# Cluster attention with a mixer: when a weight's absolute value is issued, and when U's tiles are cleared

## The chip, the cores and the metric

The kernel runs on one core of a Trainium2 chip. The metric is the device time of one execution in microseconds (us), as the median of several runs. Five engines work side by side, each through its own instructions in order: TensorE (PE, its weight loads are PEld), VectorE (DVE), ScalarE (ACT), GpSimd (POOL) and SyncE (SP), which issues every transfer of this kernel. They wait for each other by semaphores.

## What is computed

The reference in short: a clustered attention, a mixing block and a second mixing block with a feed-forward.

```
mask   = argmax(q_n @ c_n) == argmax(k_n @ c_n)           # 16 clusters a head
attn   = softmax(where(mask, q @ k.T / 8, -1e9)) @ v      # 2 x 8 heads, 768 x 64
x      = attn with the heads side by side                 # 2 x 768 x 512
theta  = x @ w_theta
u      = x + w_tok_r @ (x * cos(theta)) + w_tok_i @ (x * sin(theta))
x2     = u + relu(u @ w_ch)
u2     = x2 + (x2.T @ U @ V).T
out    = u2 + relu(u2 @ w_ch1) @ w_ch2
```

All weights come from memory as 64-bit floats and are turned into pairs of 32-bit tiles on the chip, while other work runs.

## The kernel before

**Stages.** A prologue, then attention over eight groups g0 to g7 (two heads of one batch row each), then the mixer: 24 steps that each make one block of theta (`theta`, L476), its cosine and sine, and z (`theta_z`, L496, `theta_lo`, L502), and two steps later the products with w_tok_r and w_tok_i (`ymix`, L518). Then come w_ch, U and V, and the feed-forward.

**A group** has six slots, p0 to p5. In a slot PE forms score tiles `st` for this group (L301), ACT takes their exponentials `p` (L306, four instructions a slot), and PE forms scores `smax` of the next group (L249), whose row maxima `mx` DVE reduces (L253, three a slot). Two products `pv` of exponentials and values (L314) follow, and at p1 and p5 the sums of the exponentials, `l` (L333: at p5 over the tiles of its first three key blocks, at p1 of the next group over the rest). PE works through this in the order written, and that order doesn't change.

**What is fitted in between.** At the end of a slot `fill(1.7)` issues side work until a running account, `owed`, is used up: first the items in `bg` (splitting q and k of a later group into high and low part, L186 on ACT and L191 on POOL; assigning clusters, `sims`, `amax`, `eq`, `weigh`, `least`, `onehot`, `turn`, L122 to L150 on DVE), and then steps of the conversion of a weight, `conv_step`, at a cost of 1 each.

**A weight's conversion** (`Convert`): its load by SP into a staging tile `st` (`load`, L374; two such buffers, so a new load is issued once a weight has gone through `low`); `magnitude` on ACT (absolute value, L382, `cv<-st`); `bits` (L386), `top` (L390) and `low` (L394) on DVE; then, as callbacks that are issued at the end of a slot's scores, `wh` on ACT (L399) and `wl` on POOL (L403). Before the change `magnitude` of the following weight is issued right behind `low` of the one before. During attention (`held[0]`) the order of weights is wth0 to wth2 (theta), then wr0, wi0, wr1, wi1, ... wr5, wi5.

**Buffers.** The tiles `p`, `cv`, `wh`, `wl`, `lt` and many others come from one pool of 59 slots, handed out in the program's order; a tile that takes a slot waits until the last reader of the tile that held it is done. PE's results go to eight banks in a ring, two of them kept by `pv`; a matmul that takes a bank waits for the last reader of what it held. Six banks turn round, and a slot takes three for `st` and three for `smax`, so `l` at the end of a slot takes the bank of that slot's first `st`, and can start once the first exponential of the slot has read it.

**U.** U's conversion ends in five callbacks, one to a `conv_step`: `keep_u0` clears four tiles `ub` on POOL (L560), then `keep_u` four times, each with four small copies on ACT (L567).

Of the kernel before, what the change touches and what calls it, by code (L numbers as in the profile page):

```python
# [10 lines left out]
F32 = mybir.dt.float32  # L11
# [9 lines left out]
B, H, S, D, C = 2, 8, 768, 64, 16  # L21
DM, RANK, DFF = 512, 32, 2048
P = 128
# [17 lines left out]
def tile_cluster_block(ctx: ExitStack, tc: tile.TileContext, qk, v, cent, wth, wr, wi, wch,  # L41
                       u_in, v_in, w1, w2, cst, out):
    nc = tc.nc
# [7 lines left out]
    def slot(name, dt=F32, shape=None):  # L51
        return sp.tile(shape or [P, S], dt, tag="slot", name=name)
# [265 lines left out]
    def pv_out(g):  # L318
        xT[g] = slot(f"xT{g}")
        for hf in range(2):  # L320
            nc.scalar.activation(out=xT[g][:, cols(hf)], in_=pvt[g][hf][:, :HALF], func=AF.Copy)
        give("pv")
# [35 lines left out]
    def norm_x(g):  # L358
        nc.vector.tensor_tensor(xT[g], xT[g], rl.pop(g), op=ALU.mult)


    class Convert:
# [5 lines left out]
            self.c0, self.w = i * S, min(S, n - i * S)  # L368

        def load(self):  # L370
            self.st = stg.tile([P, S, 2], I32, tag="st", name="st")
            for g in range(self.copies):
                r = slice(g * self.rows, (g + 1) * self.rows)
                nc.sync.dma_start(out=self.st[r, :self.w].rearrange("p n t -> p (n t)"),  # L374
                                  in_=self.src[:, self.c0:self.c0 + self.w].bitcast(I32))
            self.part = slice(0, self.copies * self.rows)
            self.hw, self.lw = self.st[self.part, :self.w, 1], self.st[self.part, :self.w, 0]
# [28 lines left out]

    conv_load, conv_in, conv_do, conv_after = deque(), deque(), deque(), deque()
    held = [False]

    def conv_start():  # L410
        while conv_load and len(conv_in) < 2:
            c = conv_load.popleft()
            c.load()
            conv_in.append(c)

    def conv_step(n=1):

        for _ in range(n):
            if conv_after and not held[0]:
                conv_after.popleft()()  # L420
            if not conv_do:
                conv_start()
                if not conv_in:
                    return
                c = conv_in[0]

                def last(c=c):
                    c.low()
                    conv_in.popleft()
                    conv_after.extend([lambda f=f: f(c) for f in c.done])  # L430
                    if conv_in:
                        conv_in[0].magnitude()
                    conv_start()

                conv_do.extend((c.bits, c.top, last))
                if c.t is None:
                    conv_do.appendleft(c.magnitude)
            conv_do.popleft()()

    def conv_until(dst, i):  # L440
        while i not in dst:
            assert conv_do or conv_in or conv_load or conv_after
            conv_step()
# [110 lines left out]
    ub = []  # L554
    vs = []

    def keep_u0(c):
        for i in range(4):
            t = slot(f"ub{i}", F32, [P, 6, P])
            nc.gpsimd.memset(t, 0.0)  # L560
            ub.append(t)

    def keep_u(c, g):
        z = c.t.rearrange("p (k r) -> p k r", r=RANK)
        r = slice(32 * g, 32 * g + 32)
        for i in range(4):
            nc.scalar.activation(out=ub[i][r, :, r], in_=z[r, 6 * i:6 * i + 6], func=AF.Copy)  # L567
        if g == 3:
            uv["u"] = True
# [101 lines left out]
    bg = deque()  # L671

    owed = [0.]

    def fill(t):

        owed[0] += t
        while owed[0] > 0:
            if bg:
                c, f = bg.popleft()  # L680
                f()
                owed[0] -= c
            else:
                conv_step()
                owed[0] -= 1.

    PAUSE = (1, lambda: None)

# [6 lines left out]
    def attention():  # L695


        ORDER = [(0, 0), (0, 2), (0, 4), (1, 0), (1, 2), (1, 4)]
        pvq = deque()
        held[0] = True  # L700

        def next_pv():
            g, kt, hf = pvq.popleft()
            pv(g, kt, hf)
            if kt == NT - 1 and hf:
                pv_out(g)

        for g in range(NG):
            nxt = g + 1 < NG
            if nxt:  # L710
                load_v(g + 1)
            if g + 2 < NG:
                if g > 0:
                    bg.extend(split_items(g + 2, nc.gpsimd))
                bg.extend(assign_items(g + 2))
            if g + 4 < NG:
                for i in range(2):
                    load_raw(g + 4, i)
            if g == 1:
                conv_load.extend(weigh_in(wth, NP * DM, wth_t))  # L720
                conv_start()
            if g == 2:
                tok = [c for p in zip(weigh_in(wr, NT * S, wr_t), weigh_in(wi, NT * S, wi_t)) for c in p]
                conv_load.extend(tok[:6])
                late = tok[6:]
            if g == 6:
                conv_load.extend(late)
                conv_start()
            if g in (6, 7):
                for t in range(2):  # L730
                    bg.append((0, lambda t=2 * g - 12 + t: split_x(0, t, nc.gpsimd)))
            order = [None, (1, 0), None, (1, 2), None, (1, 4)] if g == 0 else ORDER
            for p in range(NT):
                ready = len(pvq)
                if order[p]:
                    h, a = order[p]
                    scores_pair(g, h, a)
                    if h:
                        pvq.extend((g, kt, hf) for kt in (a, a + 1) for hf in range(2))
                if nxt:  # L740
                    max_pair(g + 1, p // 3, 2 * p % 6)
                    if p % 3 == 2:
                        max_join(g + 1, p // 3)

                while conv_after:
                    conv_after.popleft()()
                if p == 3 and g + 2 < NG:
                    mask_rows(g + 2)
                if g > 0 and p == 1:
                    sum_keys(g - 1, 1)  # L750
                if p == 5:
                    sum_keys(g, 0)
                for _ in range(min(ready, 2)):
                    next_pv()
                if g > 0 and p == 1:
                    row_sums(g - 1)
                if g > 0 and p == 5:
                    bg.appendleft((.95, lambda: norm_x(g - 1)))
                    bg.appendleft((.97, lambda: spread(g - 1)))
                fill(1.7 if nxt else 3.4)  # L760
                if g > 0 and p == 0:
                    max_rows(g, 1)
                if nxt and p == 3:
                    max_rows(g + 1, 0)
            while bg:
                fill(.5)
        held[0] = False
        while len(pvq) > 1:
            next_pv()
        nc.scalar.activation(out=warm, in_=warm, func=AF.Sin)  # L770
        next_pv()
        sum_keys(NG - 1, 1)
# [96 lines left out]
    def mixer():  # L869
# [4 lines left out]
        for n in range(len(seq) + LEAD):  # L874
            if n < len(seq):
                theta(*seq[n])
                conv_step()
                theta_z(*seq[n])
            if n >= LEAD:
                ymix(*seq[n - LEAD])  # L880
            if n == 1:
                row_sums(last)
            if n == 2:
                spread(last)
                norm_x(last)
            if n not in range(16, 20):
                conv_step()
            if n < len(seq):
                theta_lo(*seq[n])
            if n not in range(16, 20):  # L890
                conv_step(1)
            if n in (9, 10):
                for t in range(2):
                    split_x(1, 2 * (n - 9) + t)
            if n == 12:
                conv_load.extend(weigh_in(wch, NP * DM, wch_t))
                c1, c2 = weigh_in(w1, NF * DM, w1_t), weigh_in(w2, NF * DM, w2_t)
                conv_load.extend([c1[0], c2[0]])
                conv_load.append(Convert(u_in, S, 0, [keep_u0] + [lambda c, g=g: keep_u(c, g) for g in range(4)], 32, 4))
                conv_load.append(Convert(v_in, S, 0, [keep_v, keep_vl], 32))  # L900
                for p in zip(c1[1:], c2[1:]):
                    conv_load.extend(p)
                conv_start()
            if 20 <= n <= 23:
                split_x(0, n - 20, nc.gpsimd)
            if n in (24, 25):
                split_x(1, n - 24, nc.gpsimd)
# [101 lines left out]
```

## Time and profile before

| | |
|---|---|
| Median of three runs | 729.67 us (727.72 to 731.31) |
| Span of the profiled execution | 725.5 us, 10613 instructions |
| Busy share of the span | PE 96%, PEld 75%, DVE 60%, ACT 41%, POOL 27% |
| Granted clock of TensorE, mean | 0.988 of full speed |

The span runs from the first to the last instruction of the one execution that was profiled. The profile gives no other time of that execution; the median of the runs stands 4.2 us above its span, which holds what lies around it. An engine's share is an average over stages in which different engines wait.

### The profile page before, as it was taken

The numbers are of one execution on the slowest core, as the hardware profiler recorded it, in microseconds if no ns is written. First come the engines' busy times: TensorE is split into PE (matmuls) and PEld (weight loads), VectorE is DVE, ScalarE is ACT, GpSimd is POOL, SyncE is SP. The second block draws the span as 40 slices with busy tenths as digits, with TensorE's granted clock in tenths as the row PEclk, the third lists the DMA queues.
The fourth block names the chain that finished last, engine by engine and source line by source line (L and its number), as shares of the span: only waits on it lengthen the run. The fifth ranks groups of instructions, "written<-read, shape, count | busy, mean of one in ns | idle before, by whom it ended". The sixth has DMA issues, their size and how long they took to land.

```text
span 725.5 us, 10613 instructions
## 1 busy us (share of the span) xinstructions
PE 696.6 (96%) x4109; PEld 546.2 (75%) x4110; DVE 436.5 (60%) x746; ACT 301.0 (41%) x613; POOL 196.7 (27%) x191
## 2 busy tenths in 40 slices
PE   6699989999999899999998899999999999999997
PEld 2455554554555479999998899898888888888986
DVE  7777986878788645447677877644344453332222
ACT  5655644665667644354546712422222222110000
POOL 9602313142244722112346712321221211100000
PEclk9799999999999999999999999999999999999999
DMA  7969666465423400000222211022121221100112
GB/s 210 238 177 262 171 147 186 126 161 151 112 82 127 140 37 1 2 1 30 88 54 89 88 44 44 0 88 74 58 87 51 81 87 30 30 1 0 59 38 79
DMA packets 21506, 64.05 MB, mean 88 GB/s; under 512 B 4272, under 2 KB 6192, under 8 KB 21456
## 3 DMA queue, kind: packets, MB, share of 16 engines
q1 hardware_dynamic: 21456, 63.37, 30.5%
q8 instruction: 32, 0.52, 0.3%
q14 instruction: 18, 0.15, 0.1%
HBM read 40.94 MB, written 3.15 MB: 61 GB/s over the span
## 4 chain that ended last, share of the span: by engine, by line
PE 86%; DVE 7%; ACT 3%; issue 2%; DMA 1%; POOL 0%; SPq 0%; DVEq 0%; ACTq 0%; POOLq 0%
PE g L633 19%; PE acc L653 18%; PE y L518 11%; PE st L301 9%; PE pv L314 8%; PE l L333 5%; PE h L536 5%; PE smax L249 4%; PE th L476 4%; DVE mx L253 2%; PE h L588 1%; DMA st<-in_wr_dram 1%; DVE tht L484 1%; PE sims L119 1%; PE th L480 1%
## 5 line engine op out<-in xcount | busy, mean ns | idle before, releaser
L403 POOL TENSOR_TENSOR wl<-cv,wh 128x768 fp32r<-128x768 f32 (+1 forms) x40 | 79.3, 1982 | 223.7 <-ACT wh L399 195.9
L640 DVE SCALAR_TENSOR_TENSOR gl<-g,gh 128x512 fp32r<-128x512 f32 x48 | 33.2, 692 | 155.7 <-ACT gh L638 155.7
L638 ACT ACTIVATE gh<-g 128x512 fp32r<-128x512 f32 x48 | 28.7, 599 | 202.0 <-PE g L633 202.0
L306 ACT ACTIVATE p<-st 128x512 f32<-128x512 f32 x192 | 78.9, 499 | 65.8 <-PE st L301 59.2
L253 DVE TENSOR_REDUCE mx<-smax 128x1 f32<-128x512 f32 x144 | 90.1, 683 | 20.4 <-PE smax L249 20.4
L518 PE MATMUL y<-wh,z 128*128 128x384 f32 x384 | 89.0, 344 | 4.5 <-ACT z L496 4.5
L633 PE MATMUL g<-uh,wh 128*128 128x512 f32 (+1 forms) x256 | 86.9, 339 | 0.0
L633 PE MATMUL g<-uh,wl 128*128 128x512 f32 (+1 forms) x256 | 86.5, 338 | 0.0
L633 PE MATMUL g<-ul,wh 128*128 128x512 f32 (+1 forms) x256 | 86.1, 337 | 0.0
L301 PE MATMUL st<-qp,kp 128*128 128x256 f32 (+1 forms) x384 | 81.7, 355 | 0.5 <-ACT p L306 0.5
L301 PEld LDWEIGHTS st<-qp,kp 128*128 128x128 f32 x384 | 56.0, 191 | 26.6 <-issue 10.2
L653 PE MATMUL acc<-gh,wh 128*128 128x512 f32 x192 | 75.9, 395 | 0.0
L653 PE MATMUL acc<-gh,wl 128*128 128x512 f32 x192 | 75.6, 394 | 0.0
L653 PE MATMUL acc<-gl,wh 128*128 128x512 f32 x192 | 75.3, 392 | 0.0
L314 PE MATMUL pv<-p,v 128*64 128x384 f32 x384 | 71.6, 498 | 1.4 <-ACT p L306 1.4
L518 PEld LDWEIGHTS y<-wh,z 128*128 128x128 f32 x384 | 67.9, 191 | 5.1 <-ACT z L496 5.1
L633 PEld LDWEIGHTS g<-ul,wh 128*128 128x128 f32 x256 | 48.5, 189 | 6.5 <-POOL ul L616 0.4
L633 PEld LDWEIGHTS g<-uh,wl 128*128 128x128 f32 x256 | 48.4, 189 | 5.8
L633 PEld LDWEIGHTS g<-uh,wh 128*128 128x128 f32 x256 | 48.4, 189 | 5.7
L314 PEld LDWEIGHTS pv<-p,v 128*64 128x64 f32 x384 | 23.6, 136 | 37.6 <-issue 34.4
L518 PE MATMUL y<-wl,z 128*128 128x384 f32 x192 | 49.5, 339 | 0.0
L394 DVE SCALAR_TENSOR_TENSOR cv<-st,cv 128x768 int32<-128x768 int32 (+2 forms) x42 | 45.1, 1075 | 0.9
(129 smaller groups left out, 1177.0 us busy)
## 6 DMA issues: line engine op xcount, KB each, us to landing
st<-in_w_dram SPq DMA_DIRECT2D x20, 768.0 KB, 4.2
raw<-in_qk_dram SPq DMA_DIRECT2D x16, 384.0 KB, 4.7
qp<-hi SPq DMA_DIRECT2D x30, 192.0 KB, 3.0
st<-in_wr_dram SPq DMA_DIRECT2D x6, 768.0 KB, 4.3
st<-in_wi_dram SPq DMA_DIRECT2D x6, 768.0 KB, 4.3
kp<-hi SPq DMA_DIRECT2D x32, 96.0 KB, 3.0
qp<-lo SPq DMA_DIRECT2D x32, 96.0 KB, 2.9
v<-in_v_dram SPq DMA_DIRECT2D x8, 384.0 KB, 3.6
```

Of the source, the lines that this page charges most:

```text
L253: nc.vector.tensor_reduce(mx_t[g, h][:, o:o + n], ps.rearrange("p (n w) -> p n w", n=n), axis=AX.X, op=ALU.max)
L301: nc.tensor.matmul(out=ps[:, c:c + n], lhsT=kp[s, h, w][:, (a + j) * P:(a + j + 1) * P], rhs=qp[s, h, w][:, q0:q0 + n], start=(w == 0), st ...
L306: nc.scalar.activation(out=pt[g, h, a + j][:, q0:q0 + n], in_=ps[:, c:c + n], func=AF.Exp, scale=float(D) ** -0.5)
L314: nc.tensor.matmul(out=pvt[g][hf][64 * h:64 * h + 64, :HALF], lhsT=v_t[g][:, kt, 64 * h:64 * h + 64], rhs=pt[g, h, kt][:, hf * HALF:(hf + ...
L333: nc.tensor.matmul(out=ps[o:o + 32, :HALF], lhsT=ones, rhs=pt[g, h, kt][:, cols(hf)], start=(kt == 3 * a), stop=(kt == 3 * a + 2))
L394: nc.vector.scalar_tensor_tensor(t, self.lw, 29, t, op0=ALU.logical_shift_right, op1=ALU.bitwise_or)
L403: nc.gpsimd.tensor_tensor(t[:, :c.w], c.t, f32(c.hi[:, :c.w]), op=ALU.subtract)
L518: nc.tensor.matmul(out=yps[u, j][hf][:, :HALF], lhsT=lhs, rhs=w[st][e][:, hf * HALF:(hf + 1) * HALF], start=(st == 0 and n == 0), stop=(st ...
L536: nc.tensor.matmul(out=ps[hf][:, :HALF], lhsT=wv[a], rhs=xs[b, t][c][:, hf * HALF:(hf + 1) * HALF], start=(n == 0), stop=(n == 11))
L633: nc.tensor.matmul(out=ps[:, o:o + w], lhsT=wv[a], rhs=us[b, t][e][:, s0:s0 + w], start=(n == 0), stop=(n == 11))
L640: nc.vector.scalar_tensor_tensor(gl, ps, 0.0, f32(gh), op0=ALU.max, op1=ALU.subtract)
L653: nc.tensor.matmul(out=aps[c, e], lhsT=wv[a], rhs=g[x], start=(first and i == 0), stop=(last and i == 2))
```

## The change

Four things are done. `conv_magnitude`, at the head of every attention slot, issues the absolute value of the weight in front, if its load was issued at least two slots before (`RIPE`); behind `low` it is no longer issued while attention runs, and `conv_step` does nothing, and says so, when the front weight has no absolute value yet. `fill` then stops, and carries over at most 1 (`OWED`) of its account. The first load of w_tok, wr0, is issued at the head of g2, beside wth2. And the tiles `ub` are cleared one by one in steps 13 to 16 of the mixer, so U's callbacks are four.

```diff
         def load(self):
+            self.at = tick[0]
...
     held = [False]
+    tick = [0]
+    RIPE = 2
+
+    def conv_magnitude():
+        if conv_in and conv_in[0].t is None and tick[0] - conv_in[0].at >= RIPE:
+            conv_in[0].magnitude()
...
                 conv_start()
-                if not conv_in:
-                    return
+                if not conv_in or held[0] and conv_in[0].t is None:
+                    return False
...
                     conv_after.extend([lambda f=f: f(c) for f in c.done])
-                    if conv_in:
+                    if conv_in and not held[0]:
                         conv_in[0].magnitude()
...
             conv_do.popleft()()
+        return True
...
-    def keep_u0(c):
-        for i in range(4):
-            t = slot(f"ub{i}", F32, [P, 6, P])
-            nc.gpsimd.memset(t, 0.0)
-            ub.append(t)
+    def clear_u(i):
+        t = slot(f"ub{i}", F32, [P, 6, P])
+        nc.gpsimd.memset(t, 0.0)
+        ub.append(t)
...
+    OWED = 1.
     def fill(t):
...
+            elif conv_step():
+                owed[0] -= 1.
             else:
-                conv_step()
-                owed[0] -= 1.
+                owed[0] = min(owed[0], OWED)
+                return
...
                 late = tok[6:]
+                conv_start()
...
                 ready = len(pvq)
+                tick[0] += 1
+                conv_magnitude()
...
-                conv_load.append(Convert(u_in, S, 0, [keep_u0] + [lambda c, g=g: keep_u(c, g) for g in range(4)], 32, 4))
+                conv_load.append(Convert(u_in, S, 0, [lambda c, g=g: keep_u(c, g) for g in range(4)], 32, 4))
...
+            if 13 <= n <= 16:
+                clear_u(n - 13)
```

In the listings below a row is the line of the kernel, the operation, and output and inputs with the number of the tile; lines behind L366 stand one higher after the change (the absolute value is L382 before and L383 after).

ACT in g2, from the mask rows of p4 on, before; `st_1263` is the staging tile of wr0, the first piece of w_tok_r:

```order
L282 ACTIVATE qp001_86<-mrow_1266 2x384 x2
L306 ACTIVATE p1_1275<-st_1277 128x512
L306 ACTIVATE p1_1275<-st_1281 128x256
L306 ACTIVATE p1_1276<-st_1281 128x256
L306 ACTIVATE p1_1276<-st_1288 128x512
L399 ACTIVATE wh_1302<-cv_928 128x768
L382 ACTIVATE cv_1314<-st_1263 128x768
L306 ACTIVATE p1_1318<-st_1320 128x512
L306 ACTIVATE p1_1318<-st_1324 128x256
```

ACT at the same place after the change; wr0's staging tile is `st_1047` there, loaded at the head of the group:

```order
L282 ACTIVATE qp001_86<-mrow_1274 2x384 x2
L383 ACTIVATE cv_1283<-st_1047 128x768
L306 ACTIVATE p1_1285<-st_1287 128x512
L306 ACTIVATE p1_1285<-st_1291 128x256
L306 ACTIVATE p1_1286<-st_1291 128x256
L306 ACTIVATE p1_1286<-st_1298 128x512
L400 ACTIVATE wh_1312<-cv_981 128x512
L306 ACTIVATE p1_1324<-st_1326 128x512
```

The absolute value stood behind p4's exponentials and `wh`, ahead of p5's exponentials; it stands now at the head of p4, and the `wh` of a weight of theta between the two groups of exponentials.

DVE in g1, from the join of the maxima in p2 to the maxima of p4, before; `cv_885` is wth0, the first piece of theta's weight:

```order
L269 TENSOR_TENSOR m2_882<-mx_880,m2_882 128x6
L386 TENSOR_SCALAR cv_885<-cv_885 128x768
L253 TENSOR_REDUCE mx12_905<-smax_906 128x1
L253 TENSOR_REDUCE mx12_905<-smax_909 128x2
L253 TENSOR_REDUCE mx12_905<-smax_913 128x1
L390 SCALAR_TENSOR_TENSOR cv_885<-st_707,cv_885 128x768
L394 SCALAR_TENSOR_TENSOR cv_885<-st_707,cv_885 128x768
L253 TENSOR_REDUCE mx12_905<-smax_958 128x1
L253 TENSOR_REDUCE mx12_905<-smax_961 128x2
```

And after the change, with `cv_791` for wth0 and `cv_892` for wth1:

```order
L269 TENSOR_TENSOR m2_885<-mx_883,m2_885 128x6
L391 SCALAR_TENSOR_TENSOR cv_791<-st_707,cv_791 128x768
L395 SCALAR_TENSOR_TENSOR cv_791<-st_707,cv_791 128x768
L253 TENSOR_REDUCE mx12_911<-smax_912 128x1
L253 TENSOR_REDUCE mx12_911<-smax_915 128x2
L253 TENSOR_REDUCE mx12_911<-smax_919 128x1
L387 TENSOR_SCALAR cv_892<-cv_892 128x768
L391 SCALAR_TENSOR_TENSOR cv_892<-st_709,cv_892 128x768
L253 TENSOR_REDUCE mx12_911<-smax_964 128x1
```

One conversion step stood ahead of p3's maxima (`smax_906` to `smax_913`) and two behind them; now two stand ahead (`smax_912` to `smax_919`) and two behind.

ACT in g4, p4 and the beginning of p5, before; `cv_1987` and `cv_1889` are wi1 and wr1, `p1_1991` the first exponentials of p5:

```order
L306 ACTIVATE p1_1954<-st_1959 128x256
L306 ACTIVATE p1_1954<-st_1966 128x512
L382 ACTIVATE cv_1987<-st_1891 128x768
L306 ACTIVATE p1_1991<-st_1993 128x512
L306 ACTIVATE p1_1991<-st_1997 128x256
L306 ACTIVATE p1_1992<-st_1997 128x256
L306 ACTIVATE p1_1992<-st_2004 128x512
L399 ACTIVATE wh_2023<-cv_1889 128x768
```

And after the change; `cv_1956` is wi1, `cv_1660` wr1, and `p1_1997` the first exponentials of p5, whose slot is the one that `cv_1660` held:

```order
L383 ACTIVATE cv_1956<-st_1658 128x768
L306 ACTIVATE p1_1958<-st_1960 128x512
L306 ACTIVATE p1_1958<-st_1964 128x256
L306 ACTIVATE p1_1959<-st_1964 128x256
L306 ACTIVATE p1_1959<-st_1971 128x512
L400 ACTIVATE wh_1985<-cv_1660 128x768
L306 ACTIVATE p1_1997<-st_1999 128x512
L306 ACTIVATE p1_1997<-st_2003 128x256
```

wi1's absolute value moved ahead of p4's exponentials, and wr1's `wh` from behind p5's exponentials to ahead of them; POOL's `wl` of wr1 reads `cv_1660` behind that `wh`.

## Rows read from the trace of the kernel before

**Rows 1.** the page: span, and shares of the chain that ended last

```profile
span 725.5 us, 10613 instructions
...
PE 86%; DVE 7%; ACT 3%; issue 2%; DMA 1%; POOL 0%; SPq 0%; DVEq 0%; ACTq 0%; POOLq 0%
```

**Rows 2.** timeline, all engines, 108 to 112 us: start, length, instruction [idle before <-releaser]

```profile
109.04 0.89 ACT L382 ACTIVATE cv<-st 128x768 f32<-128x768 f32 x1 [4.14 <-DMA st<-in_wr_dram]
...
110.46 3.84 PE L333 MATMUL l<-p,ones 128*32 128x384 f32 x24 [3.74 <-ACT p L306]
```

**Rows 3.** windows: stretch, busy (x) PE PEld DVE ACT POOL, PEclk, DMA, GB/s

```profile
110.40:114.30 3.90, 3.84 (x26) 1.08 (x28) 0.00 (x0) 1.56 (x5) 1.26 (x1) 0.56 0.96 387
```

**Rows 4.** chain in order of time, g0: start, length, engine, line

```profile
45.43 1.81 DVE mx L253 x3
```

**Rows 5.** timeline of DVE in g0

```profile
47.76 0.57 DVE L150 STREAM_TRANSPOSE eqw<-eqw 128x384 bf16<-128x384 bf16 x1
```

**Rows 6.** timeline of g1, 70 to 82 us

```profile
72.84 1.88 DVE L253 TENSOR_REDUCE mx<-smax 128x1 f32<-128x512 f32 x3
...
74.64 0.95 DVE L390 SCALAR_TENSOR_TENSOR cv<-st,cv 128x768 int32<-128x768 int32 x1
...
75.06 1.51 PE L314 MATMUL pv<-p,v 128*64 128x384 f32 x8
...
78.30 1.57 DVE L386 TENSOR_SCALAR cv<-cv 128x768 int32<-128x768 int32 x1
```

**Rows 7.** timeline of g4, 144 to 172 us

```profile
146.64 3.63 POOL L191 TENSOR_TENSOR lo<-raw,hi 128x768 fp32r<-128x768 f32 x2 [5.78 <-ACT hi L186]
...
150.38 2.14 PE L333 MATMUL l<-p,ones 128*32 128x384 f32 x24
...
163.97 1.64 ACT L306 ACTIVATE p<-st 128x512 f32<-128x512 f32 x4
...
167.69 2.14 PE L333 MATMUL l<-p,ones 128*32 128x384 f32 x24
...
168.73 1.81 POOL L403 TENSOR_TENSOR wl<-cv,wh 128x768 fp32r<-128x768 f32 x1 [5.63 <-ACT wh L399]
```

**Rows 8.** timeline of g5, 165 to 190 us

```profile
178.77 0.56 DVE L130 TENSOR_TENSOR eqw<-s_t,mxc 128x384 bf16<-128x384 f32 x1 [0.62 <-POOL lo L191]
...
180.07 2.14 PE L333 MATMUL l<-p,ones 128*32 128x384 f32 x24 [1.72 <-ACT p L306]
```

**Rows 9.** timeline of g6, 214 to 228 us

```profile
216.90 1.88 DVE L253 TENSOR_REDUCE mx<-smax 128x1 f32<-128x512 f32 x3
...
218.21 1.83 POOL L403 TENSOR_TENSOR wl<-cv,wh 128x768 fp32r<-128x768 f32 x1 [3.85 <-issue]
...
218.69 2.17 DVE L390 SCALAR_TENSOR_TENSOR cv<-st,cv 128x768 int32<-128x768 int32 x1
...
224.97 2.14 PE L333 MATMUL l<-p,ones 128*32 128x384 f32 x24
```

**Rows 10.** chain in order of time, g7

```profile
238.34 0.23 DVE rl L343
...
240.44 4.12 DMA st<-in_wr_dram
```

**Rows 11.** timeline of g7

```profile
240.29 0.55 DVE L386 TENSOR_SCALAR cv<-cv 128x768 int32<-128x768 int32 x1
...
246.02 1.51 PE L314 MATMUL pv<-p,v 128*64 128x384 f32 x8 [1.36 <-ACT p L306]
```

**Rows 12.** timeline of the mixer's steps 21 to 23

```profile
388.49 3.35 POOL L560 MEMSET ub<- 128x768 f32 x4
...
391.07 0.73 ACT L496 ACTIVATE z<-tht 128x256 fp32r<-128x256 f32 x2 [0.75 <-DVE tht L493]
...
391.71 2.24 ACT L567 ACTIVATE ub<-cv 32x192 f32<-32x192 f32 x8
...
400.90 1.01 PE L518 MATMUL y<-wh,z 128*128 128x384 f32 x2 [4.21 <-ACT z L496]
```

## The prediction

> **What bounds the kernel now.** I read the page first. The chain of work that ended last is 86% PE [rows 1]: over most of the 725.5 us PE is never short of work, and nothing done beside it counts. So the change is worth what it does to the few places where PE waits, and I went through attention group by group with the timeline to find these, then through the chain of waits to see what ended each. The largest by far is in g2 at p5. ACT's absolute value of wr0 stood idle for 4.14 us for its load, and p5's exponentials stand behind it on ACT. PE's `l` needs the bank that the first of them frees, so it waited 3.74 us [rows 2]. Behind that wait the granted clock of the stretch was 0.56, near the lower level of 1.2 GHz [rows 3], and this `l` took 3.84 us where the one of g4 takes 2.14 [rows 2, 7]. Smaller ones: 1.72 in g5 [rows 8], 1.36 in g7 [rows 11], and 4.21 in the mixer's step 23 [rows 12]. In g0 the chain goes through DVE's maxima [rows 4].
>
> I then put the rows of the change's order against these times: which instruction stands ahead of which, what held the slot or the bank that an instruction takes, and when that came free.
>
> **The change part by part.** Nothing is computed more or less, except that the four clears are on other steps. Everything is a question of who stands in front of whom.
>
> A, g2 p5. wr0 is now loaded at the head of g2 and its absolute value issued at p4's head, four slots behind. The wait goes, and the slow `l` with it: 3.74 + (3.84 - 2.14) = **-5.4**. If a wait of the size of those in g5 or g7 comes in its place, -3.7; nothing suggests more than -5.4.
>
> B, g0. The account starts one higher, so the item `turn` (0.57, [rows 5]) moves ahead of the maxima of p2, which are on the chain there [rows 4]: **+0.5**, from 0 to 0.6.
>
> C, g1. The assignment's items stand in p0 now but for one, and wth0's conversion begins a slot earlier. So `top` and `low` of wth0, 0.95 each [rows 6], stand ahead of p3's maxima where `bits` (0.55, [rows 11]) stood: 1.35 more. DVE also reaches this place some 0.3 later, since the items drawn forward push its work for `l` and p2's maxima back (an estimate: they are a little over 1 us, and most of it is idle time of DVE there). Before, those of p3 ended at 72.84 + 1.88 = 74.72, and p4's `pv`, which takes the bank of the third of them, started at 75.06 [rows 6]. The maxima would end at 74.72 + 1.65 = 76.4 and `pv` start then: +1.3. Behind it `bits` and `top` of wth1 stand ahead of p4's maxima, the first stretched to 1.57 beside POOL's `wl` as it was at 78.30 [rows 6], which puts p5's `smax` back by another 0.7 (1.57 + 0.95 ahead of maxima that stood free, less what `st` of p5 and PE's own delay cover, some 1.8). Together **+2.0**. The low end is 0.2, if the banks have more slack than this counting gives; the high end 2.6.
>
> D, g4 p1. The first exponential now takes a slot that POOL's second `lo` reads last, until 146.64 + 3.63 = 150.27. With the 0.5 that the first exponential of a group of four needs (estimate from 1.64 for four) `l` could start at 150.8 and started at 150.38 [rows 7]: **+0.4**, from 0 to 0.6.
>
> E, g4 p5. The first exponential takes the slot of wr1's `cv`, whose `wh` now stands right ahead of it and whose `wl` is POOL's. p4's exponentials end at 163.97 + 1.64 = 165.6, `wh` takes 0.9 like the absolute value of [rows 2], `wl` 1.81, the exponential 0.5: 168.8, against `l` at 167.69 [rows 7]. **+1.2** with the hand-over between engines, from 0 (PE itself late by then) to 1.6.
>
> F, g5 p1. The first exponential waited for the slot that DVE's `eq` read; `eq` had itself waited for POOL's `lo` and took 0.56 from 178.77 [rows 8]. After the change that slot waits for `lo` alone: **-0.6**. At best the whole wait of 1.72 goes, at worst nothing.
>
> G, g6 p5. wr4's load is issued behind `low` of wr3, which now stands behind p3's maxima. These end at 216.90 + 1.88 = 218.8 [rows 9], I take 219.0; `low` is done at 220.0. The load lands 4.12 later, like the one of [rows 10], at 224.1; 0.9 of absolute value at p5's head and 0.5 of exponential make 225.5, against `l` at 224.97 [rows 9]: **+0.6**, from 0 to 1.6. Here the rule "two slots old" does not help: p3 to p5 is two slots, and they last less than load and conversion.
>
> H, g7. The chain before runs from DVE's sums over wr/wi conversions into the load of the last weight, 4.12 [rows 10], and PE's `pv` waits 1.36 [rows 11]. After the change wi4's three steps begin when the sums are through, at 238.6 [rows 10], and take 0.55 + 0.95 + 0.95: the load leaves at 241.1 instead of 240.44 and lands at 245.2. The absolute value stands at p3's head and blocks ACT as before, so the wait becomes about 2.0. Some of the 0.6 comes back, since no further absolute value stands ahead of p4's exponentials: **+0.3**, from -1.8 (no wait at all) to +0.9.
>
> I, the mixer. Clearing cost POOL 3.35 for four [rows 12], and PE did not wait for it. In steps 13 to 16 the clears lie in POOL's idle time, one a step, 0.8 each. But U's callbacks come one `conv_step` sooner: half of the eight copies of 2.24 us, 1.1, now stand on ACT ahead of step 22's z, where ACT was idle for only 0.75 [rows 12]. The rest, 0.4, is passed on to step 23, whose wait of 4.21 becomes 4.6: **+0.4**, from -0.3 to +0.8. That wait itself is not touched.
>
> Sum: -5.4 + 0.5 + 2.0 + 0.4 + 1.2 - 0.6 + 0.6 + 0.3 + 0.4 = **-0.6**. The span of 725.5 becomes 724.9. The median of the runs stands 4.2 above the span of the profiled execution, so about **729.1**: the one big wait goes, and small ones take its place. With all terms at their low ends the sum is -8.9, at their high ends +5.0.
>
> **The rule that speaks against it.** At 218.69 DVE's `top` took 2.17, where the same instruction takes 0.95 elsewhere [rows 6, 9]; POOL's `wl` of 1.83, begun at 218.21, ran beside it [rows 9]. The Trainium skill says ("SBUF — State Buffer", section "SBUF: two separate sides") that DVE and GpSimd share one pair of ports as an exclusive lock, so the one that starts second stands for the other's whole instruction; the 2.17 agrees with that. In G, plain durations give +0.6; a step blocked as at 218.69 would issue the load up to 1.2 later, about half of it in time in which DVE would wait anyway (an estimate), so +1.2, and the sum would be 0.0 instead of -0.6.
>
> **The rivals.**
>
> 1. *The new waits don't bite.* Slots and banks have more slack than the counting gives, DVE makes up in its idle time, and only A and F remain: -6.0, **723.7**. For it: each of B to E is 2 us or less, and each is counted from the ends of single instructions. Against it: g0 and g1 have DVE on the chain already [rows 4], and D and E follow from one buffer's last reader.
>
> 2. *Slower: POOL's `wl` becomes the last reader in front of the exponentials.* Place: g4 p5 (E). If `wl` of wr1 starts late or is stretched by DVE's `bits` and `top` beside it, by 1.22 for each as at 218.69 (2.17 against 0.95, [rows 9]), the wait grows from 1.2 to 3.6. The point from which it decides is a wait as long as that of g2, behind which the clock fell: then the 1.7 of a slow `l` comes on top, 3.6 + 1.7 = 5.3 instead of 1.2. Sum -0.6 + 4.1 = +3.5: **733.2**. For it: the order puts `wh`, `wl` and exponential in one line. Against it: it needs both stretches at once.
>
> 3. *DVE is blocked by POOL throughout,* as at 218.69, wherever a step now stands beside a `wl`: G at 1.2, B and C at their high ends (0.6 and 2.6). Sum -0.6 + 0.6 + 0.1 + 0.6 = +0.7: **730.4**. The rule above is of this kind.
>
> 4. *The wait of g2 only moves:* wr0's absolute value is no longer late, but wi0's or wr1's is, at a head of a slot. Then A is -3.7 and the sum +1.1: **730.8**.
>
> **How the numbers follow.** I give the sum 0.45, the first rival 0.27, the second 0.08, the third 0.12, the fourth 0.08. A difference of 0.5%, 3.65 us, is about what a measurement of this kernel can tell from no change (its runs lie 3.6 apart). Faster than that: the first rival and a little of the sum's low side, 0.30; slower: the second and a little of the high side, 0.10; within: 0.60. The range reaches down to the first rival and up to near the second: 723.5 to 733.0; the sum's own is 726.5 to 732.
>
> **What would show it.** In the changed kernel's timeline PE's `l` in g2 p5 should have no wait and take 2.14 (A). p4's `pv` in g1 should start 1.4 later measured from the same slot's `st` (C). `l` of g4 p5 should name ACT's exponential, and that one POOL's `wl`, as what it waited for, by about 1.2 us (E). `l` of g6 p5 should wait for an exponential behind an absolute value that waited for its load (G), and the load of wi5 still be on the chain in g7 (H). The wait at step 23 should be 4.6 (I). I am wrong if the sum of PE's waits in g1, g4 and g6 is near nothing: then it is the first rival, and the banks and slots were freed earlier than their order says. I am wrong on the other side if a stretch with a low granted clock appears from g4 on.

## The result, and the profile after

The changed kernel took **732.62 us** (median of four runs, 731.89 to 733.63) beside 729.32 for the kernel before: a ratio of 1.0053, 95% interval 1.003 to 1.0076. The forecast was 729.1, a little faster; it became slower by half a per cent, inside the range and on the other side.

Of the changed kernel's runs the spans are known as well, and each lies 1.8 below its time (730.9 of 732.68 in the profiled one), so the 4.2 that the prediction put around the span was too much: the profiled execution of before, 725.5, must have taken about 727.3, the low end of its spread. The two profiles are 5.4 apart, the medians 3.3; what follows compares the two profiled executions with each other. Of 68 executions of the kernel before that ran beside the experiments, the 35 with a mean granted clock of 0.988, as in the profiled one, have a median of 727.9, and the 33 with a lower one 729.6, so the missing 2 goes with the clock; in which stretch it falls isn't shown.

PE's order is the same in both kernels, so the starts of its sixteen `l` show where time went. The first fence is the timeline of PE in the changed kernel (start, length, instruction, wait and what ended it), cut to `l` of g2 p5, g4 p1 and p5, g5 p1, g6 p5 and g7 p5:

```profile
110.06 2.14 PE L333 MATMUL l<-p,ones 128*32 128x384 f32 x24
...
148.93 2.14 PE L333 MATMUL l<-p,ones 128*32 128x384 f32 x24 [0.58 <-ACT p L306]
...
167.85 2.14 PE L333 MATMUL l<-p,ones 128*32 128x384 f32 x24 [1.54 <-ACT p L306]
...
179.61 2.14 PE L333 MATMUL l<-p,ones 128*32 128x384 f32 x24 [1.07 <-ACT p L306]
...
226.13 2.14 PE L333 MATMUL l<-p,ones 128*32 128x384 f32 x24 [1.52 <-ACT p L306]
...
254.02 2.14 PE L333 MATMUL l<-p,ones 128*32 128x384 f32 x24
```

The `l` of g2 p5 has lost its wait of 3.74 and takes 2.14 [rows 2]. But that of g4 p5 waits 1.54, that of g6 p5 1.52, and the one of g4 p1 0.58, where before none of the three waited [rows 7, 9]. Against the same places of before:

| stretch, up to the start of `l` in | before | after | difference so far | of this stretch | term, predicted |
|---|---|---|---|---|---|
| g1 p1 | 64.50 | 65.95 | +1.45 | +1.45 | B +0.5 |
| g1 p5 | 78.87 | 82.28 | +3.41 | +1.96 | C +2.0 |
| g2 p5, and g3 p1 behind its `l` | 110.46, 122.61 | 110.06, 120.52 | -0.40, -2.09 | -5.50 | A -5.4 |
| g4 p1 | 150.38 | 148.93 | -1.45 | +0.64 | D +0.4 |
| g4 p5 | 167.69 | 167.85 | +0.16 | +1.61 | E +1.2 |
| g5 p1 | 180.07 | 179.61 | -0.46 | -0.62 | F -0.6 |
| g6 p5 | 224.97 | 226.13 | +1.16 | +1.62 | G +0.6 |
| g7 p5 | 249.83 | 254.02 | +4.19 | +3.03 | H +0.3 |
| the end of the span | 725.5 | 730.9 | +5.4 | +1.2 | I +0.4 |

Every row has the sign that was forecast. Against the high ends of the prediction, H is 2.1 over, B 0.85 and I 0.4; A, C, D, E, F and G end within 0.1 of their bounds. In g7 the timeline of the changed kernel shows, in order, DVE's transpose `lt` of the key sums, the three steps of wi4, the last load (wi5), the absolute value that waits for it, the exponential and PE's `pv`:

```profile
239.55 0.58 DVE L336 STREAM_TRANSPOSE lt<-l 128x384 f32<-128x384 f32 x1 [3.25 <-PE st L301]
...
241.14 0.50 DVE L387 TENSOR_SCALAR cv<-cv 128x768 int32<-128x768 int32 x1
...
241.67 0.96 DVE L391 SCALAR_TENSOR_TENSOR cv<-st,cv 128x768 int32<-128x768 int32 x1
242.66 0.96 DVE L395 SCALAR_TENSOR_TENSOR cv<-st,cv 128x768 int32<-128x768 int32 x1
...
243.69 0.33 SPq L375 DMA_DIRECT2D st<-in_wi_dram  x1
...
248.01 0.89 ACT L383 ACTIVATE cv<-st 128x768 f32<-128x768 f32 x1 [3.45 <-DMA st<-in_wi_dram]
248.80 1.62 ACT L306 ACTIVATE p<-st 128x512 f32<-128x512 f32 x4
...
249.44 1.80 PE L314 MATMUL pv<-p,v 128*64 128x384 f32 x8 [3.61 <-ACT p L306]
```

And the windows around that wait's end (busy time and number of PE, PEld, DVE, ACT, POOL, then granted clock, DMA share and GB/s):

```profile
249.40:254.00 4.60, 4.56 (x16) 2.50 (x16) 2.01 (x3) 4.08 (x11) 1.93 (x1) 0.63 0.39 106
```

`lt` starts at 239.55, behind 3.25 of idle time that a matmul of the next slot's scores ended, though its own `l` had run from 234.56 for 2.14. So the last load is issued at 243.69, the absolute value waits 3.45 for it, and `pv` 3.61, where before it waited 1.36 [rows 11]. Behind that wait the granted clock is 0.63: TensorE fell towards 1.2 GHz as it had in g2 before [rows 3]. Of the 3.03, the longer wait is 2.25; the rest, 0.77, is the slower matmuls behind it, less the 0.45 that `l` of g7 p5 waited before and no longer does. More than half of what the change won in g2 is lost again in g7.

### The profile page after: what moved, and what is told of

Read it like the earlier page. It is cut to its first block, busy times and chain, and to the rows that moved or that the text cites. A ratio compares the mean times of both kernels' runs of the same rounds, so it can differ in the third digit from the quotient of the medians.

```text
span 730.9 us, 10616 instructions
## 1 busy us (share of the span) xinstructions
PE 700.5 (96%) x4109; PEld 548.3 (75%) x4110; DVE 440.8 (60%) x746; ACT 301.8 (41%) x613; POOL 195.0 (27%) x191
## 4 chain that ended last, share of the span: by engine, by line
PE 68%; DVE 3%; ACT 3%; issue 2%; DMA 1%; POOL 0%; DVEq 0%; ACTq 0%; POOLq 0%; SPq 0%
PE g L641 18%; PE acc L661 18%; PE y L527 11%; PE h L545 5%; PE th L485 4%; PE pv L314 4%; PE st L301 3%; PE l L333 2%; PE h L596 1%; DVE tht L493 1%; PE smax L249 1%; DMA st<-in_wi_dram 1%; PE th L489 1%; ACT ub L575 1%; DMA st<-in_wr_dram 1%
## 5 line engine op out<-in xcount | busy, mean ns | idle before, releaser
L301 PE MATMUL st<-qp,kp 128*128 128x256 f32 (+1 forms) x384 | 83.4, 361 | 0.5 <-ACT p L306 0.5
L301 PEld LDWEIGHTS st<-qp,kp 128*128 128x128 f32 x384 | 57.5, 196 | 27.4 <-issue 11.4
L249 PE MATMUL smax<-kp,qp 128*128 128x512 f32 x192 | 43.4, 346 | 2.0 <-POOL kp L207 1.2
```

The source lines that it names most:

```text
L249: nc.tensor.matmul(out=ps[:, c:c + w], lhsT=qp[s, h, 0][:, (a + j) * P:(a + j + 1) * P], rhs=kp[s, h, 0][:, k0:k0 + w], start=True, stop=True)
L301: nc.tensor.matmul(out=ps[:, c:c + n], lhsT=kp[s, h, w][:, (a + j) * P:(a + j + 1) * P], rhs=qp[s, h, w][:, q0:q0 + n], start=(w == 0), st ...
```

## The experiments

Each ratio is against runs of the kernel before on the same chip, whose median was 728.95 beside the first four experiments, 728.32 beside the next four and 728.59 beside the last three.

### The account as before

```diff
-            elif conv_step():
-                owed[0] -= 1.
             else:
-                owed[0] = min(owed[0], OWED)
-                return
+                conv_step()
+                owed[0] -= 1.
```

> The changed kernel with the account of fill as before (it pays 1 for a step that finds nothing to do, nothing is clamped). Theory: what g0 and g1 lost in the changed trace (1.45 up to g1 p1 and 1.96 more up to g1 p5) comes from the higher account, which draws DVE work ahead of the maxima; most of it comes back, about 2.5 of 3.4: 730. Rival: the loss is made in g7 whatever g0 and g1 do, since everything behind only slides: 732 to 733, with the long wait in g7 still there.

**724.90** (723.32 to 725.82), ratio 0.9941 (0.9929 to 0.9954). Far more came back than expected. PE's timeline, `l` of g1 p1, g4 p1, g4 p5, g5 p1, g6 p5 and g7 p5:

```profile
65.62 2.14 PE L333 MATMUL l<-p,ones 128*32 128x384 f32 x24 [1.00 <-ACT p L306]
...
146.70 2.14 PE L333 MATMUL l<-p,ones 128*32 128x384 f32 x24
...
164.01 2.14 PE L333 MATMUL l<-p,ones 128*32 128x384 f32 x24
...
174.47 2.14 PE L333 MATMUL l<-p,ones 128*32 128x384 f32 x24
...
219.13 2.14 PE L333 MATMUL l<-p,ones 128*32 128x384 f32 x24
...
244.11 2.14 PE L333 MATMUL l<-p,ones 128*32 128x384 f32 x24 [0.45 <-ACT p L306]
```

No `l` waits in g4, at g5 p1 and at g6 p5, and g7 is nearly as before: `pv` waits 1.49 and `l` 0.45. So D, E and G came from the account, and so did the extra wait of g7. Of the 3.41 of B and C, which the theory was about, only 1.58 came back: `l` of g1 p5 starts at 80.70, still 1.83 behind before. At g1 p1 `l` waits 1.00, because p1's exponentials stand behind wth0's absolute value, now at that slot's head, and that one waits 0.67 for its load. The rival, that g7 loses whatever the groups ahead do, is out. Up to step 23 of the mixer this kernel loses 1.8 against before; the last weight's `top` and `low` run there, at 257.89 and 259.77, behind the end of attention.

### The clears alone

```diff
-                conv_load.append(Convert(u_in, S, 0, [keep_u0] + [lambda c, g=g: keep_u(c, g) for g in range(4)], 32, 4))
+                conv_load.append(Convert(u_in, S, 0, [lambda c, g=g: keep_u(c, g) for g in range(4)], 32, 4))
...
+            if 13 <= n <= 16:
+                clear_u(n - 13)
```

This is the kernel before with these lines.

> The kernel before with only U's clears moved to steps 13 to 16 (attention untouched). Theory: four copies now stand ahead of step 22's z, the last theta wait grows by 0.2 to 0.4, and the y behind it is slowed by up to 1.0 more: 729.5 to 730.7. Rival one: the clears cost nothing: 729.3. Rival two: they carry the whole loss: 732.6.

**728.06** (727.28 to 729.72), ratio 0.9994 (0.9983 to 1.0005): no difference, and no loss, 1.4 below what was expected. The first rival holds: the clears carry none of the 3.3. The wait of step 23 does grow by the 0.24, to 4.45, but that doesn't show in the time.

### Attention's part alone

The changed kernel with the clears back in `keep_u0` (the lines above undone).

> The changed kernel with U's clears as before, so attention's part alone. Theory: 732.6 less 0.2 to 1.2, 731.4 to 732.4. Rival: attention alone is no slower than before, 729.3 or less.

**732.02** (729.63 to 733.27), ratio 1.0039 (1.0025 to 1.0053), as expected. The loss is attention's.

### A buffer of its own for g7's `lt`

```diff
-        lt = slot("lt")[:, :HALF]
+        lt = (const.tile([P, HALF], F32, name="lt7") if (g, a) == (NG - 2, 1) else slot("lt")[:, :HALF])
```

> The changed kernel; only the tile lt of g7 p1 has a buffer of its own and takes no slot. Theory: in the changed trace this lt starts 2.9 after its sums are done, because its slot is let go by PE only behind the next scores; DVE stands behind it, the last load leaves late, PE waits 3.61 and runs 1.3 slower behind that. Without it the load leaves 2.5 or more earlier, the wait falls to about 1 and the clock stays up: 732.6 less 3 to 4, 728.6 to 729.6. Rival: the order of the conversion steps alone makes the load late, and lt only fills time in which DVE would wait: 732 to 733, the wait in g7 still above 3.

**730.65** (728.99 to 731.89), ratio 1.0014 (1.0004 to 1.0024): 2.0 back by the medians and 2.2 by the two profiles, half of what was expected and not the rival's nothing. The timeline of g7, with `lt`, POOL's `wl`, `low`, the last load and PE's `pv`:

```profile
236.50 0.58 DVE L336 STREAM_TRANSPOSE lt<-l 128x384 f32<-128x384 f32 x1 [0.46 <-PE l L333]
...
238.77 2.34 POOL L404 TENSOR_TENSOR wl<-cv,wh 128x768 fp32r<-128x768 f32 x1 [1.06 <-ACT wh L400]
...
239.45 2.47 DVE L395 SCALAR_TENSOR_TENSOR cv<-st,cv 128x768 int32<-128x768 int32 x1
...
241.99 0.33 SPq L375 DMA_DIRECT2D st<-in_wi_dram  x1
...
247.46 2.16 PE L314 MATMUL pv<-p,v 128*64 128x384 f32 x8 [1.91 <-ACT p L306]
```

The windows behind its wait:

```profile
247.40:249.60 2.20, 2.14 (x9) 0.60 (x9) 2.13 (x3) 2.20 (x7) 0.36 (x1) 0.68 0.24 98
249.60:252.00 2.40, 2.40 (x10) 1.91 (x8) 0.06 (x1) 1.72 (x5) 1.74 (x1) 0.58 0.54 133
```

`lt` now starts at 236.50, right behind its sums. But `low`, the step that lets the last load go, took 2.47 beside POOL's `wl` (2.34), so the load left at 241.99: 1.7 earlier, not 2.5. `pv` still waits, 1.91, and the clock falls behind that too, to 0.68 and 0.58. From `l` of g6 p5 to that of g7 p5 this kernel takes 1.32 more than before, where the changed one takes 3.03 more: the slot of `lt` is worth 1.7 of the loss in g7.

### The account set back once, at the head of g1

```diff
             nxt = g + 1 < NG
+            if g == 1:
+                owed[0] -= 1.04
```

> The changed kernel with 1.04 taken off the account once, at the head of g1, so that g1 starts where it started before the change; g0 and g7 keep the new account. Theory: what g1 inherits from g0 sets the order of all groups behind it, so the waits in g4 p1, g4 p5, g5 p1 and g6 p5 go as they did with the old account; only g0's 1.2 and something in g7 stay: 725 to 727.5. Rival: the account inside the groups, not its start, makes these waits: 731 to 732.6.

**725.14** (723.80 to 726.02), ratio 0.9951 (0.9932 to 0.9971). One subtraction, and PE's timeline shows no wait in g4 p1, g4 p5 and g6 p5. The `l` of these places and of g5 p1, and the `pv` of g7:

```profile
147.75 2.14 PE L333 MATMUL l<-p,ones 128*32 128x384 f32 x24
...
165.06 2.14 PE L333 MATMUL l<-p,ones 128*32 128x384 f32 x24
...
176.80 2.14 PE L333 MATMUL l<-p,ones 128*32 128x384 f32 x24 [1.07 <-ACT p L306]
...
221.98 2.14 PE L333 MATMUL l<-p,ones 128*32 128x384 f32 x24
...
243.48 1.51 PE L314 MATMUL pv<-p,v 128*64 128x384 f32 x8 [1.81 <-ACT p L306]
```

The theory holds for g4 and g6: what g1 inherits from g0 makes D, E and G. It fails at g5 p1, where `l` keeps the 1.07 of the changed kernel and had no wait with the old account. In g7 the wait is 1.81, half of the changed kernel's, though g7 has the new account.

### The old account up to g6, the new one in g7

```diff
+            elif tick[0] > 6 * (NG - 1):
+                owed[0] = min(owed[0], OWED)
+                return
             else:
-                owed[0] = min(owed[0], OWED)
-                return
+                owed[0] -= 1.
```

> The old account up to g6, the new one in g7 alone. Theory: the last weight is through before the mixer, whose first steps lose 1.8 in the trace with the old account; g7 itself stays near 1.5 of wait: 723 to 724.9. Rival: the new account in g7 is what makes PE wait 3.6 there: 728 or more.

**724.14** (722.75 to 725.52), ratio 0.9941 (0.9926 to 0.9957). The new account does no harm in g7: `pv` waits 1.55 there. Against the old account throughout the medians differ by 0.8, within the spread. The last weight's `low` is now done before attention ends, but the mixer still loses 1.3 up to step 23, where the kernel with the old account throughout loses 1.8 and the changed one 0.2; so that theory holds in part at most.

### The old account and a buffer for `lt`

The edits of the first and the fourth experiment together.

> The old account, and a buffer of its own for lt of g7 p1. Theory: this lt already starts right behind its sums with the old account, so nothing is gained: 724.4 to 725.4. Rival: slots are short all through g7, and one slot more gives 1 or more: below 724.

**725.02** (723.70 to 725.70), ratio 0.9941 (0.9922 to 0.9961): nothing gained, as expected. A buffer for `lt` helps only where the rotation hands `lt` a slot that is let go late.

### One absolute value elsewhere

The kernel before, where nothing but wr0's absolute value is issued at another place:

```diff
-                    if conv_in:
+                    if conv_in and conv_in[0] is not later[0]:
                         conv_in[0].magnitude()
...
                 late = tok[6:]
+                later[0] = tok[0]
+            if g == 3:
+                later[0].magnitude()
```

> The kernel before, with one instruction elsewhere: wr0's absolute value is issued at the head of g3 and not behind the second weight of theta's last step in g2. No account, no other order changes. Theory: the wait of g2 p5 and the slow l behind it are worth 5.4 alone, and all that the change lost it lost elsewhere: 728.95 less 5 to 5.6, 723.4 to 724. Rival: the time is handed back in g3 to g7, where the loads then come late against PE: 726 or more.

**724.32** (722.67 to 725.70), ratio 0.9941 (0.9918 to 0.9963). In its profiled execution (725.7, the slowest of its six runs) it gains 3.81 at `l` of g2 p5 and 1.69 in the slow `l` behind it, and holds that to the end of attention: 4.68 ahead at g3 p1 and 4.73 at the last `l`, less than 5.50 only because g0 and g1 were 0.82 behind, with the order of before. So A is worth 5.5 by itself in attention, with one instruction moved; the median is 0.3 above the expected range.

The same profile shows, in the mixer's step 21, something that the others don't. DVE's rounding of theta (L485 here) and POOL's clears beside it:

```profile
381.96 4.64 DVE L485 TENSOR_SCALAR tht<-tht 128x256 f32<-128x256 f32 x1
...
383.68 2.78 POOL L561 MEMSET ub<- 128x768 f32 x4
```

It took 4.64, to the end of POOL's clears, where it takes 1.93 in the profile of before. PE waits 1.70 for it at the next y. So this place can hold DVE up by 2.7 in one execution and not in another; one execution shows it, no more.

### One absolute value elsewhere, and the clears

The edits of the last experiment and those of the clears, on the kernel before.

> The kernel before with two edits: wr0's absolute value at the head of g3, and U's clears in steps 13 to 16. Theory: 5.4 from g2 as before, and the clears no longer stand where DVE can be held up behind them in step 21 (the profiled run of the kernel with only the absolute value moved shows 4.64 for an instruction of 1.9 there): 723 to 724, spread smaller. Rival: the clears' place gives nothing: 724.3.

**723.49** (723.06 to 724.05), ratio **0.9923** (0.9906 to 0.9940): the fastest of all here, some 9 below the changed kernel, with the smallest spread, 1.0. In its profile the rounding has no clears beside it and takes 1.94:

```profile
382.17 1.94 DVE L485 TENSOR_SCALAR tht<-tht 128x256 f32<-128x256 f32 x1
```

That the clears gain 0.8 over the experiment before lies within the spread of that one, and alone they gave no difference; a gain from them isn't shown.

### Nothing carried over

```diff
-    OWED = 1.
+    OWED = 0.
```

> The changed kernel with OWED 0 for 1: nothing is carried over a fill that ran out of work. Theory: g1 then starts at 0, next to where it started before, so all but g0's part of the loss goes: 724.5 to 726. Rival: only a start below zero helps, the account's 0.5 in the prologue is what counts: 729 or more.

**725.83** (724.37 to 727.85), ratio 0.9957 (0.9938 to 0.9976). One constant of the changed kernel makes it faster than before, as expected. No `l` waits in g4 and at g6 p5. In g7 `pv` waits 1.96 and takes 1.62, and the granted clock is 0.80 in the 2.2 us from 243.8 on and 0.50 in the next 2.2.

### A buffer of its own for wr1's converted tile

```diff
-            self.t = slot("cv")[self.part, :self.w]
+            own = self.src is wr and self.i == 1
+            self.t = (const.tile([P, S], F32, name="cv1") if own else slot("cv"))[self.part, :self.w]
```

> The changed kernel; only wr1's converted tile has a buffer of its own, so no exponential of g4 p5 takes a slot that wl reads. Theory: the 1.54 of wait before l in g4 p5 goes, everything behind slides by as much as g5 to g7 don't take back: 730.5 to 732. Rival: wh, ahead of the exponentials on ACT, makes the wait, and it stays: 732.6.

**729.66** (727.97 to 729.82), ratio 1.0006 (0.9992 to 1.0019), 3.0 below the changed kernel, 0.8 more than expected. PE's timeline, `l` of g4 p1, g4 p5 and g6 p5, then `pv` of g7:

```profile
148.07 2.14 PE L333 MATMUL l<-p,ones 128*32 128x384 f32 x24
...
165.38 2.14 PE L333 MATMUL l<-p,ones 128*32 128x384 f32 x24
...
223.42 2.14 PE L333 MATMUL l<-p,ones 128*32 128x384 f32 x24 [1.33 <-ACT p L306]
...
246.65 2.79 PE L314 MATMUL pv<-p,v 128*64 128x384 f32 x8 [3.54 <-ACT p L306]
```

The window behind that wait:

```profile
246.60:249.40 2.80, 2.75 (x9) 0.77 (x9) 2.03 (x3) 2.80 (x7) 0.96 (x1) 0.52 0.11 46
```

Both waits of g4 are gone, with the order on every engine unchanged: the tile takes no slot from g3 on, so each later tile gets the slot of its neighbour, and the exponentials of g4 p1 lose their late reader as well. The rival is out: `wh` stands ahead of the exponentials as it did. G and the long wait of g7 (3.54, the clock at 0.52 behind it) remain.

## Why the prediction was wrong

The sum was -0.6; the two profiles say +5.4. Of these 6.0, H makes 2.7, G 1.0, B 0.95, I 0.8, D and E 0.65 together. That the time of 732.62 lies only 3.5 above the forecast is luck: the 4.2 that was put around the span was 2.4 too much. By the prediction's own terms:

**A was right** in mechanism and size: -5.50 for -5.4, here and alone.

**B was mis-sized**, +1.45 for +0.5. `turn` took its 0.58 ahead of p2's maxima, as forecast. Another 0.6 came from the transpose of the cluster scores, which started at 41.00 and not at 40.43; why stays open. So the `l` of g0 starts at 55.20 for 54.04. In the four kernels with the changed order in g0 and g1 (this one, attention alone, and the two with one more buffer) it starts at 54.99 to 55.20, with the order of before at 54.04 to 55.48, so part of this may be the execution. The last 0.3 is a path that the prediction didn't have: wth0's absolute value at the head of g1 p1, behind which `l` waits 0.21 here and 1.00 with the account of before.

**C was right**: +1.96 for +2.0. DVE and PE in the changed kernel's g1:

```profile
73.81 0.95 DVE L391 SCALAR_TENSOR_TENSOR cv<-st,cv 128x768 int32<-128x768 int32 x1
...
74.80 0.96 DVE L395 SCALAR_TENSOR_TENSOR cv<-st,cv 128x768 int32<-128x768 int32 x1
...
75.67 1.88 DVE L253 TENSOR_REDUCE mx<-smax 128x1 f32<-128x512 f32 x3
...
77.47 1.53 DVE L387 TENSOR_SCALAR cv<-cv 128x768 int32<-128x768 int32 x1
...
77.61 1.54 PE L314 MATMUL pv<-p,v 128*64 128x384 f32 x8
```

`top` and `low` stand ahead of p3's maxima, and `pv` comes at 77.61, 2.55 later than in [rows 6], of which 1.45 was there before. `bits` is stretched to 1.53 as forecast. But the account is not all of it: with the account of before, g1 still takes 0.7 longer from p1 to p5.

**D, E and F were right in kind.** F is exact (-0.62). D and E were low by 0.2 and 0.4, and the slot's last reader is shown to be their cause by the buffer for wr1. In D the first exponential names POOL's `lo` as what it waited for (148.28, behind 1.17 of idle time). The chain of E, in ACT's and POOL's rows, with the exponential that `wl` releases; the `l` behind it, at 167.85, is in the first fence of the result:

```profile
164.00 0.87 ACT L400 ACTIVATE wh<-cv 128x768 fp32r<-128x768 f32 x1
...
165.00 2.17 POOL L404 TENSOR_TENSOR wl<-cv,wh 128x768 fp32r<-128x768 f32 x1 [9.25 <-ACT wh L400]
...
167.20 1.64 ACT L306 ACTIVATE p<-st 128x512 f32<-128x512 f32 x4 [2.33 <-POOL wl L404]
```

Of the 0.4, 0.36 is `wl`, which took 2.17 and not 1.81.

**G was mis-sized**, +1.62 for +0.6. The term took the end of p3's maxima from the profile of before. There a short cast, `low` and `bits` stood ahead of them:

```profile
215.26 0.18 DVE L268 CAST m<-mx 128x6 bf16<-128x6 f32 x1
...
215.56 0.95 DVE L394 SCALAR_TENSOR_TENSOR cv<-st,cv 128x768 int32<-128x768 int32 x1
...
216.43 0.55 DVE L386 TENSOR_SCALAR cv<-cv 128x768 int32<-128x768 int32 x1
```

In the changed kernel `bits` and `top` of wr3 stand there, just as long, but POOL's `wl` runs beside the cast:

```profile
214.26 1.83 POOL L404 TENSOR_TENSOR wl<-cv,wh 128x768 fp32r<-128x768 f32 x1
...
214.84 1.29 DVE L268 CAST m<-mx 128x6 bf16<-128x6 f32 x1
...
216.25 0.55 DVE L387 TENSOR_SCALAR cv<-cv 128x768 int32<-128x768 int32 x1
...
216.84 0.96 DVE L391 SCALAR_TENSOR_TENSOR cv<-st,cv 128x768 int32<-128x768 int32 x1
...
217.71 1.88 DVE L253 TENSOR_REDUCE mx<-smax 128x1 f32<-128x512 f32 x3
...
219.51 0.95 DVE L395 SCALAR_TENSOR_TENSOR cv<-st,cv 128x768 int32<-128x768 int32 x1
...
220.54 0.33 SPq L375 DMA_DIRECT2D st<-in_wr_dram  x1
...
224.70 0.90 ACT L383 ACTIVATE cv<-st 128x768 f32<-128x768 f32 x1 [1.51 <-DMA st<-in_wr_dram]
```

The cast took 1.29 for 0.18, to 216.13, where `wl` ends at 216.09. That put the maxima at 217.71, though PE was 0.42 ahead of before, and `low` at 219.51, 0.9 later against PE than the term had it. The other three kernels with this order show the same, a cast of 1.28 or 1.29 beside `wl` and a wait of 1.33 to 1.45. So the rule that the prediction weighed here, the shared ports of the Trainium skill ("SBUF — State Buffer", section "SBUF: two separate sides"), which had the sum at 0.0, was right for G, at an instruction that the prediction hadn't priced: this `low` took its 0.95, and the cast stood beside `wl`. The trace of the experiment with the buffer for `lt` agrees with it once more: `low` in g7 took 2.47 beside `wl`.

**H is the step that failed.** H had it that "the wait becomes about 2.0", +0.3 and at most +0.9: it became 3.61, and +3.03 with the clock. The mechanism was the one named, the last load behind wi4's steps. (The load at 240.44 that the term calls the last weight's is wr5's, by its `in_wr`; wi5's comes behind it. The sum used its length, and that holds.) Two things were put at nothing. The term took the start of DVE's sums from the profile of before, but the tile `lt` got another slot in the rotation, one that PE let go only in the next slot's scores; a buffer of its own brings the load forward by 1.7 and the wait down to 1.91, near the 2.0 that the term had. And a wait of this length costs clock: the price of the wait had only been its length. With the account set back at g1 the same code in g7 waits 1.81 with no loss of clock, so H hangs on what the groups ahead hand over. The sign that the prediction named for this side, a stretch with a low granted clock from g4 on, is there: 0.63 in g7.

**I was right in kind and the rest is noise of the clock.** The wait of step 23 became 4.45 for 4.21, +0.24 for +0.4, and the clears make it: alone they give 4.45, and attention's part alone has 4.21. The y behind it took 7.03 for 5.99, at a granted clock of 0.60 for 0.72; with the wait at 4.45 or 4.46 it took 5.79 to 7.15 in the other kernels, so this 1.0 doesn't belong to the change. And against the prediction's "PE did not wait for it", a clear can stand in DVE's way, as one execution showed.

Of the rivals none came true as a whole. The first, slack everywhere, is refuted: the losses of B to E and G to I are all there. The second put the slower end in g4 p5; the price it named, a wait long enough for the clock to fall, was paid in g7. The third, DVE blocked by POOL, was right for G.

Behind most of this lies one thing that the prediction saw and counted only twice, in B and C: that the account starts one higher. By the costs in the program it stands at 1.00 at g1's head, and stood at -0.04 before; that shifts later steps to other slots. It makes D, E, G and the extra wait of H, but only about half of B and C, of whose 3.41 the account of before leaves 1.83. Set back there it gives 725.1, cut to 0 it gives 725.8, kept as before 724.9; each of these is faster than before, since D, E, G and most of H's loss are gone and A stays. That the raised account alone would make the kernel before slower wasn't tried.

## What to carry to other kernels

Where side work is issued by a running account, an offset in it is an edit of every place behind: list all steps that it moves, and time each from the new order, not from where its neighbour ended before. A rotating pool makes the last reader of a slot part of that order, and one tile more or less changes it for all that follow; a wait that comes and goes for no reason in the instructions is looked for there. And when one wait is to be removed, move that one instruction first: here it gave 724.3, as much as the best variant of the whole change, 724.1, does within the spread.

## What the runs showed that was not expected

- In attention, TensorE's clock fell behind waits of 1.91 us (0.68, then 0.58 in the stretches behind), 1.96 (0.80, then 0.50) and 3.53 to 4.03 (0.50 to 0.63), while behind waits of 1.24 to 1.81 `pv` kept its 1.51. A wait that grows from 1.4 to 2 can cost more than the 0.6.
- Instructions of DVE ran on until POOL's beside them ended: the cast in g6, 1.29 for 0.18, in all four kernels whose order puts it beside `wl`; `low` in g7, 2.47 beside `wl` and 0.96 in the changed kernel; and the rounding in step 21, 4.64 in one execution, where it met the clears, and 1.93 in the profile of before, with the same order of instructions.
